# A convolution feeding a mixture of experts on one core: blocks of inner units taken in pairs over two PSUM banks for the tiles of chunks 6 to 21, and TensorE's subtraction kept to chunks 0 to 4

## The chip, the cores and the metric

The kernel runs on one core of a Trainium2 chip. The metric is the device time of one execution in microseconds (us). Engines are called as the profile calls them: PE is TensorE, DVE is VectorE, ACT is ScalarE, POOL is GpSimd, SP is SyncE.

## The reference

There are 8 x 3584 = 28672 tokens of width D = 192. First each token becomes a weighted sum over itself and the six tokens ahead of it (a convolution with its own seven weights for each token and head). Then the token is sent to one of eight experts, and the expert's output is scaled by the gate:

```
w = exp(w - max(w)); w /= sum(w)                      # 7 taps per token and head
x[s, h] = sum over k of w[s, h, k] * x_in[s - 6 + k, h]
logits = x @ w_gate                                    # 8 experts
e = argmax(logits);  p = softmax(logits)[e]
y = p * (relu(x @ w1[e]) @ w2[e])                      # 192 -> 1024 -> 192
```

## The kernel before

**Two halves that run side by side.** The tokens are cut into 28 chunks (numbers 0 to 27) of 1024 tokens. For each chunk the *convolution half* multiplies and adds the taps (`tap_ops`: rows named tv and acc at L386 and L410, nearly all of it on DVE from chunk 5 on), splits the sums into two float16 parts (`split`: pl at L498 and L500 on DVE, transposes L506 on PE, copies xg L508 on ACT), computes logits (L518 on PE), routes (`finish`: about twenty small DVE instructions, rank matmuls L545 and L547 on PE) and scatters each token's row into its expert's queue in DRAM (L589 on POOL). Each chunk then fixes which rows the next *tiles* take (`choose`, `rows` L615). A tile is up to 384 tokens of one expert. From chunk 5 on a chunk sets free two or three tiles.

**The expert half** (`experts`) takes one tile at a time. SP reads the tile's row number and fetches its tokens (xt), the expert's weights (wt) and the gate values (meta). The 1024 inner units are 8 blocks (NF) of 128. For each block of a tile of 384, PE runs five matmuls into a PSUM bank (ph, L890), ACT takes the relu as float16 (hh, L910), and the rest of the float32 value, relu(ph) - hh, is stored as a second float16 (hl). There are two ways to get hl. In the *DVE way* (`lo`) DVE computes it from ph and hh (L913). In the *PE way* (`rest`) PE subtracts hh in the bank with one more matmul per block (negi, L903), and ACT takes the relu of what is left (L905; hh is then at L899). The second layer (`l2`) is 24 matmuls for each 128 tokens (L787, 72 for a tile of 384); they belong to the tile before the current one and are issued between the current tile's blocks. ACT scales the result (o, L791) and POOL scatters it to the output.

**PSUM.** Of eight banks, four hold `ps_h`: the blocks ph, and also the transposes of `split`, take turns in them. One bank holds the weights wp of the taps, one (`ps_m`, pm) the logits and ranks, two (`ps_o`) the second layer's sums.

**Order.** DVE's instructions stand in the order in which the program writes them. A planner in the launch code keeps two clocks, `clock[0]` for DVE and `clock[1]` for PE; DVE steps of the convolution half are issued while DVE's clock is behind, and an hl is issued once its planned time is due, or at the latest when more than three wait (`pend`). A tile's start is not planned before the time at which its rows were chosen plus 16 us (FETCH). `finish` of a chunk is planned to begin REST1 = 6 us after its transposes. PE's and ACT's orders are those that the scheduler chose when the program was built. All five orders are fixed in the built program.

In the kernel before, the PE way is used for the tiles of chunks 0 to 5, and for every eighth tile of chunks 18 to 24.

Of the kernel before, what the change touches and what calls it, by code (L numbers as in the profile page):

```python
# [10 lines left out]
F32 = mybir.dt.float32  # L11
F16 = mybir.dt.float16
# [7 lines left out]
P = 128  # L20
# [3 lines left out]
NF = F // P  # L24
# [95 lines left out]
def conv_moe_kernel(ctx: ExitStack, tc: tile.TileContext, x, wgen, w_gate, w1, w2, out):  # L120
# [17 lines left out]
    pay = conv_pools.enter_context(tc.tile_pool(name="pay", bufs=1, side="right"))  # L138
    ps_h = ctx.enter_context(tc.tile_pool(name="ps_h", bufs=4, space=bass.MemoryType.PSUM))
    ps_w = ctx.enter_context(tc.tile_pool(name="ps_w", bufs=1, space=bass.MemoryType.PSUM))  # L140
    ps_m = ctx.enter_context(tc.tile_pool(name="ps_m", bufs=1, space=bass.MemoryType.PSUM))
    start_pools = ExitStack()
    ps_y = start_pools.enter_context(tc.tile_pool(name="ps_y", bufs=2, space=bass.MemoryType.PSUM))

# [348 lines left out]
    def low(c):  # L493
# [341 lines left out]

    pend = []
    lates = []

    def experts():
# [4 lines left out]
        left = 0  # L844
        subs = []
        loaded = {}
# [18 lines left out]
        while True:  # L865
# [10 lines left out]
            hl = ffh.tile([P, NF, T], F16, name="hl", padded_shape=[P, NF, T_MAIN])  # L876
            fg = max(g for g in (1, 2, 4, 8) if g * T <= 512 or g == 1)
            groups = NF // fg
            for t in range(groups):
# [3 lines left out]
                flush()  # L883
                while len(pend) > 3:
                    low_part()
                ph = ps_h.tile([P, fg, T], F32, name="ph")
                for g in range(fg):
                    f = f0 + g
                    for k, (wc, xc) in enumerate(((0, 0), (0, 2), (O_L0, 0), (O_H1, 1), (O_L1, 1))):
                        nc.tensor.matmul(ph[:, g], wt[:, wc + f * P:wc + (f + 1) * P], xt[:, xc, 0:T],  # L890
                                         start=(k == 0 and g == 0), stop=(k == 4),
                                         skip_group_check=g > 0)
                hv, lv = hh[:, f0:f0 + fg], hl[:, f0:f0 + fg]
                while subs:
                    subs.pop(0)()
                if ((n % 8 == 1 and todo[n][3] >= LATE_SUBS) or todo[n][3] < SUBS) and todo[n][3] < NCH - 3:


                    nc.scalar.activation(hv, ph, AF.Relu, scale=SHRINK)  # L899

                    def rest(ph=ph, hv=hv, lv=lv, fg=fg):
                        for g in range(fg):
                            nc.tensor.matmul(ph[:, g], negi, hv[:, g], start=False, stop=True,  # L903
                                             skip_group_check=True)
                        nc.scalar.activation(lv, ph, AF.Relu)  # L905
# [3 lines left out]
                else:  # L909
                    nc.scalar.activation(hv, ph, AF.Relu)  # L910

                    def lo(ph=ph, hv=hv, lv=lv):
                        nc.vector.scalar_tensor_tensor(lv, ph, 0.0, hv, op0=ALU.max, op1=ALU.subtract)  # L913
                        return (T * fg + 60) / 960.0

                    cost = T * fg * (5 + 4.5) / 2400.0 + 14 * fg * MM
                    clock[1] += cost
                    pend.append((clock[1] + LATE, n, lo))
# [6 lines left out]
                if t == groups - 1:  # L925
                    p = min(P, T)
# [7 lines left out]
            while subs:  # L934
                subs.pop(0)()
            second(10 ** 6)
# [9 lines left out]
    def last_tiles():  # L946

        loads = [fetch(len(todo) + i) for i in range(2)]
        for i in range(len(rest)):
# [9 lines left out]
            for f0 in range(0, NF, fg):  # L959
                ph = ps_h.tile([P, fg, T], F32, name="ph")  # L960
                for g in range(fg):
# [15 lines left out]
    def low_part():  # L977
        at, _, lo = pend.pop(0)
        clock[0] = max(clock[0], at) + lo()
# [101 lines left out]
    start_pools.close()  # L1081
    ps_o = ctx.enter_context(tc.tile_pool(name="ps_o", bufs=1, space=bass.MemoryType.PSUM))
    for i in range(2):
# [49 lines left out]
```

## Time and profile before

| | us |
|---|---|
| median of 3 runs | 1186.59 (1183.4 to 1188.95) |
| the profiled execution | 1185.47 |
| its span, first to last instruction | 1183.8 |
| PE busy | 1123.8 (95%) |
| DVE busy | 1034.9 (87%) |
| POOL busy | 696.3 (59%) |
| ACT busy | 647.1 (55%) |

Busy time is the sum of an engine's recorded instructions without overlap. Matmuls are pipelined: one is recorded longer than the distance to the start of the next, so a PE that shows no idle time may still be read only by counting its matmuls.

### The profile page before, as it was taken

What the parts mean: (1) busy time and instruction counts of PE and PEld (TensorE: products, weight loads), DVE (VectorE), ACT (ScalarE), POOL (GpSimd) and SP (SyncE); (2) the same over time, 40 slices, a digit from 0 to 9 for tenths busy, and PEclk for the clock granted to TensorE, in tenths of its full rate; (3) what the DMA queues carried; (4) which work ended last, traced back from release to release, by engine and by line L of the source; (5) the groups of instructions that cost most, each with busy time, mean ns of one, the idle gap of its engine ahead of it and who ended that gap; (6) DMA issues with size and microseconds to landing.
All of it is one profiled execution on the core that took longest, in us unless ns stands there. A gap on an engine that the chain in (4) does not pass through costs nothing. (4 is left out here: it accounts for less than half of the span.)

```text
span 1183.8 us, 29289 instructions
## 1 busy us (share of the span) xinstructions
PE 1123.8 (95%) x11327; PEld 913.1 (77%) x11327; DVE 1034.9 (87%) x1771; ACT 647.1 (55%) x1348; POOL 696.3 (59%) x633
## 2 busy tenths in 40 slices
PE   5689799999999999999999999999999999999996
PEld 3455489998778878787788888787777777778996
DVE  7999999999999999999999999999999997833231
ACT  3555477777556555545554555656465556443342
POOL 7998647766654654664566566447555675721222
PEclk9999899999999999999999999999999999999999
DMA  9989899999889787888898788777687666799993
GB/s 280 378 299 335 248 335 308 307 307 307 254 219 279 239 257 229 258 240 232 221 290 237 209 276 260 234 209 236 235 242 245 196 151 223 235 330 353 351 344 136
DMA packets 182847, 311.44 MB, mean 263 GB/s; under 512 B 131243, under 2 KB 154785, under 8 KB 167470
## 3 DMA queue, kind: packets, MB, share of 16 engines
q1 hardware_dynamic: 160702, 264.17, 73.3%
q0 software_dynamic: 22000, 45.33, 12.0%
q8 instruction: 91, 1.49, 0.5%
q14 instruction: 54, 0.44, 0.1%
HBM read 226.97 MB, written 60.45 MB: 243 GB/s over the span
## 5 line engine op out<-in xcount | busy, mean ns | idle before, releaser
L890 PE MATMUL ph<-xt,wt 128*128 128x384 f16 (+6 forms) x3680 | 571.2, 296 | 9.5 <-DVE hl L913 5.5
L787 PE MATMUL yo<-wt,hh 128*128 128x192 f16 (+1 forms) x3648 | 489.8, 246 | 2.9 <-ACT o L791 2.9
L589 POOL DMA_INDIRECT out_dram<-o,meta x228 | 281.1, 1233 | 323.5 <-ACT o L791 254.5
L787 PE MATMUL yo<-wt,hl 128*128 128x192 f16 (+1 forms) x1824 | 438.3, 246 | 0.0
L890 PEld LDWEIGHTS <-wt 128*128 128x128 f16 x3680 | 317.7, 98 | 124.3 <-issue 6.4
L910 ACT ACTIVATE hh<-ph 128x384 f16<-128x384 f32 (+2 forms) x485 | 238.5, 495 | 292.9 <-PE ph L890 272.1
L913 DVE SCALAR_TENSOR_TENSOR hl<-ph,hh 128x384 f16<-128x384 f32 (+2 forms) x485 | 260.4, 552 | 110.7 <-ACT hh L910 110.2
L787 PEld LDWEIGHTS <-hh 128*128 128x128 f16 (+1 forms) x3648 | 330.2, 98 | 32.9 <-issue 3.7
L589 POOL DMA_INDIRECT queue<-pl,pos x224 | 289.7, 1293 | 98.6 <-issue 72.9
L386 DVE TENSOR_TENSOR tv<-x_sb,wp 128x1536 f32<-128x1536 f32 (+1 forms) x173 | 286.2, 1656 | 1.7 <-PE ph L395 1.4
L410 DVE TENSOR_TENSOR acc<-acc,tv 128x1536 f32<-128x1536 f32 x138 | 239.6, 1736 | 0.0
L787 PEld LDWEIGHTS <-hl 128*128 128x128 f16 (+1 forms) x1824 | 178.7, 98 | 18.5 <-ACT hl L905 0.2
L791 ACT ACTIVATE o<-yo,fac 128x192 f32<-128x192 f32 (+1 forms) x228 | 90.5, 418 | 89.5 <-PE yo L787 85.1
L508 ACT ACTIVATE xg<-ph 128x1024 f16<-128x1024 f16 x84 | 81.6, 1022 | 38.2 <-PE ph L506 38.0
L395 PE MATMUL ph<-tv,identf 128*128 128x384 f32 x210 | 82.6, 539 | 17.8 <-DVE tv L386 17.1
L395 PEld LDWEIGHTS ph<-tv,identf 128*128 128x128 f32 x210 | 41.4, 209 | 45.2 <-DVE tv L386 19.0
L899 ACT ACTIVATE hh<-ph 128x512 f16<-128x512 f32 (+1 forms) x88 | 48.9, 562 | 22.1 <-PE ph L890 16.0
L447 ACT ACTIVATE junk<-x_sb 128x768 bf16<-128x768 f32 (+2 forms) x56 | 48.0, 857 | 16.1 <-DVE ssq L456 6.0
L905 ACT ACTIVATE hl<-ph 128x512 f16<-128x512 f32 (+1 forms) x88 | 47.7, 559 | 10.6 <-PE ph L903 10.2
L506 PE MATMUL ph<-idh,pl 128*128 128x128 f16 x672 | 52.3, 219 | 0.4 <-DVE pl L500 0.3
L486 ACT ACTIVATE pl<-acc 128x768 f16<-128x768 f32 (+1 forms) x51 | 39.0, 805 | 15.3 <-DVE acc L410 9.2
L506 PEld LDWEIGHTS <-pl 128*128 128x128 f16 x672 | 42.7, 98 | 5.9 <-ACT pl L491 2.6
(133 smaller groups left out, 768.9 us busy)
## 6 DMA issues: line engine op xcount, KB each, us to landing
wt<-wq SPq DMA_DIRECT2D x92, 1796.0 KB
x_sb<-in_x_dram SPq DMA_DIRECT2D x27, 1344.0 KB
w_sb<-in_weight_gen_dram SPq DMA_DIRECT2D x28, 224.0 KB
wq<-ws SPq DMA_DIRECT2D x8, 772.0 KB
f<-in_moe_w_dram SPq DMA_DIRECT2D x8, 768.0 KB
f<-in_moe_w_dram SPq DMA_DIRECT2D x8, 512.0 KB
wq<-ws SPq DMA_DIRECT2D x8, 512.0 KB
wq<-ws SPq DMA_DIRECT2D x32, 128.0 KB
```

The source lines that it names most:

```text
L386: eng.tensor_tensor(out, xs, ws, op=ALU.mult)
L395: nc.tensor.matmul(ap[:, 0:m], identf, tf[:, 2 * i * D:2 * i * D + m], start=(n == 0), stop=(n == KW - 1))
L410: eng.tensor_tensor(ac, ac, t, op=ALU.add)
L506: nc.tensor.transpose(pt[:, m, :], p16[:, j, n * P:(n + 1) * P], idh)
L508: nc.scalar.activation(k.xg[:, i:i + 8, :], pt, AF.Copy)
L589: st = nc.gpsimd.indirect_dma_start(out=dst, out_offset=bass.IndirectOffsetOnAxis(ap=idx, axis=0), in_=src, in_offset=None, **kw)
L787: nc.tensor.matmul(y, hx[:, f, sl], w2v[:, f, t, :], start=(f == 0 and k == 0), stop=(f == NF - 1 and k == 2))
L791: nc.scalar.activation(o[0:m, :], y, AF.Copy, scale=fac[0:m, s:s + 1])
L890: nc.tensor.matmul(ph[:, g], wt[:, wc + f * P:wc + (f + 1) * P], xt[:, xc, 0:T], start=(k == 0 and g == 0), stop=(k == 4), skip_group_chec ...
L899: nc.scalar.activation(hv, ph, AF.Relu, scale=SHRINK)
L910: nc.scalar.activation(hv, ph, AF.Relu)
L913: nc.vector.scalar_tensor_tensor(lv, ph, 0.0, hv, op0=ALU.max, op1=ALU.subtract)
```

## The change

Tiles of chunks 6 to 21 take two blocks at a time. A buffer is then a pair of banks (two pairs instead of four single banks), PE fills it with ten matmuls, ACT takes one relu over 768 columns and DVE one hl over 768 columns. Tiles of other chunks keep one bank at a time. The pools change over at the first tile of chunk 6 and at the first tile of chunk 22. While pairs are in use, the transposes go through the single bank of pm, and `finish` is planned 13 us (REST2) after the transposes instead of 6. The PE way is kept for chunks 0 to 4 alone. Rules for the order of l2's matmuls and of waiting hl's are adapted. Line numbers rise: L910 becomes L936, L913 becomes L939, L386 and L410 become L390 and L414, L508 becomes L513.

```diff
-SUBS = 6
-LATE_SUBS = 18
+SUBS = 5
+PAIRS_FROM = 6
+PAIRS_TO = 22
+REST2 = 13.0
...
         for i in range(0, len(blocks), 8):
-            pt = ps_h.tile([P, 8, P], F16, name="ph")
+            pt = (ps_m.tile([P, 8, P], F16, name="pm") if len(pairs) == 1 else
+                  (pairs[-1] if pairs else ps_h).tile([P, 8, P], F16, name="ph"))
...
-        yield max(0.0, ch[c].sent + REST1 - clock[0])
+        yield max(0.0, ch[c].sent + (REST2 if len(pairs) == 1 else REST1) - clock[0])
...
-            fg = max(g for g in (1, 2, 4, 8) if g * T <= 512 or g == 1)
+            sub_all = todo[n][3] < SUBS
+            stage_ = (todo[n][3] >= PAIRS_FROM) + (todo[n][3] >= PAIRS_TO)
+            if stage_ > len(pairs):
+                while pend:
+                    low_part()
+                flush_subs()
+                h_pools.close()
+                pairs.append((h_pools if stage_ == 1 else ctx).enter_context(tc.tile_pool(name=f"ps_d{stage_}", bufs=2 * stage_,
+                                                                space=bass.MemoryType.PSUM)))
+            nb = 2 if len(pairs) == 1 else 1
+            per = max(g for g in (1, 2, 4) if g * T <= 512 or g == 1)
+            fg = min(NF, per * nb)
...
-                while len(pend) > 3:
+                while len(pend) > 4 // nb - 1:
                     low_part()
...
-                if ((n % 8 == 1 and todo[n][3] >= LATE_SUBS) or todo[n][3] < SUBS) and todo[n][3] < NCH - 3:
+                if sub_all:
...
-                if t > 0 or groups == 1:
-                    while pend and pend[0][1] < n:
+                if t > 0 or groups == 1 or nb == 2:
+                    m = -(-left // (groups - t))
+                    if t == 0 and groups > 1:
+                        m = min(m, 3 * ready)
+                    while pend and pend[0][1] < n and (3 * ready < m or t > 0 or pend[0][3]):
                         low_part()
-                    m = -(-left // (groups - t))
```

In the stretch with pairs, ACT's order shows what became of the relu's and of the transposes. Here are ACT's rows late in that stretch in the changed program (hh and its bank ph, o with the second layer's bank yo, xg copied out of pm):

```order
L936 ACTIVATE hh_12377<-ph_12440 128x768
L796 ACTIVATE o_12458<-yo1_1337,fac_12183 128x192
L513 ACTIVATE xg_12474<-pm_12475 128x1024
L936 ACTIVATE hh_12377<-ph_12515 128x768
L513 ACTIVATE xg_12474<-pm_12485 128x1024
L796 ACTIVATE o_12539<-yo1_1337,fac_12183 128x192
L936 ACTIVATE hh_12377<-ph_12555 128x768
```

Before, each of these relu's was two rows of 128x384, and the three copies xg of a chunk read ph and stood next to each other; now they read pm, one after another in the same bank, with other work between them.

The second place is the third tile after the change back to single banks, which is also the first tile of the next chunk's rows. These are DVE's rows around the first hl of that tile (hl_14473) in the program before; acc and tv are the convolution of 1536 columns:

```order
L913 SCALAR_TENSOR_TENSOR hl_14201<-ph_14435,hh_14200 128x384
L534 SCALAR_TENSOR_TENSOR pri_14466<-lg_14409,revE_101 128x64
L459 TENSOR_SCALAR ssi_14468<-ssq_14461 128x1
L410 TENSOR_TENSOR acc_14146<-acc_14146,tv_14411 128x1536
L537 TENSOR_REDUCE pmx_14484<-pri_14466 128x8
L463 TENSOR_SCALAR rsx_14486<-ssi_14468 128x1
L386 TENSOR_TENSOR tv_14488<-x_sb_12894,wp_14147 128x1536
L540 TENSOR_TENSOR oh0_108<-pri_14466,pmx_14484 128x64
L554 TENSOR_REDUCE se_14551<-eg0_112 128x8
L466 TENSOR_SCALAR lsc_14553<-ssi_14468,gofs_172 128x1
L410 TENSOR_TENSOR acc_14146<-acc_14146,tv_14463 128x1536
L913 SCALAR_TENSOR_TENSOR hl_14473<-ph_14477,hh_14472 128x384
```

And these are DVE's rows at the same tile (its hl is hl_13967) in the changed program, with the middle of the stretch left out:

```order
L939 SCALAR_TENSOR_TENSOR hl_13638<-ph_13822,hh_13637 128x384
L414 TENSOR_TENSOR acc_13707<-acc_13707,tv_13817 128x1536
L939 SCALAR_TENSOR_TENSOR hl_13638<-ph_13840,hh_13637 128x384
L530 TENSOR_REDUCE lg_13891<-pm_13866 128x64
L390 TENSOR_TENSOR tv_13893<-x_sb_12418,wp_13708 128x1536
L533 TENSOR_REDUCE lm_13895<-lg_13891 128x8
L414 TENSOR_TENSOR acc_13707<-acc_13707,tv_13860 128x1536
...
L390 TENSOR_TENSOR tv_13984<-x_sb_12418,wp_13708 128x1536
L575 TENSOR_TENSOR rk_13980<-rk_13980,oh0_108 128x64
L370 RECIPROCAL sm_13978<-sm_13978 128x64
L414 TENSOR_TENSOR acc_13707<-acc_13707,tv_13913 128x1536
L939 SCALAR_TENSOR_TENSOR hl_13967<-ph_13971,hh_13966 128x384
```

Before, ten rows, three of them tv or acc, stand between the last hl of one tile and the first of the next. Now 27 rows stand there, from lg to acc: eight of them are tv or acc, and nineteen are small instructions of a chunk's routing and weights.

## Rows read from the trace of the kernel before

**Rows 1.** Busy time by stretch: the stretch, its length, then for PE, PEld (weight loads), DVE, ACT and POOL the busy us and in brackets the number of instructions, then the granted TensorE clock, the DMA share and GB/s.

```profile
core 0: us, PE busy (x) PEld busy (x) DVE busy (x) ACT busy (x) POOL busy (x), PEclk, DMA share, GB/s
0.00:150.00 150.00, 111.10 (x725) 71.24 (x726) 133.81 (x237) 74.55 (x125) 125.96 (x161) 0.94 0.93 309
...
240.00:400.00 160.00, 160.00 (x1652) 134.18 (x1650) 159.29 (x266) 100.77 (x216) 98.79 (x81) 1.00 0.92 268
400.00:600.00 200.00, 199.72 (x1982) 159.97 (x1980) 196.06 (x332) 109.17 (x237) 112.92 (x96) 1.00 0.83 241
600.00:810.00 210.00, 209.93 (x2076) 168.27 (x2075) 205.60 (x340) 117.51 (x254) 126.66 (x99) 1.00 0.83 249
810.00:970.00 160.00, 153.78 (x1536) 122.25 (x1534) 156.97 (x260) 88.42 (x187) 98.10 (x78) 1.00 0.70 211
970.00:1184.00 214.00, 200.90 (x2350) 174.66 (x2348) 96.26 (x210) 90.09 (x204) 76.77 (x77) 0.99 0.87 279
```

**Rows 2.** What PE waited for between 810 and 970 us: the waiting line, what it waited for, us in total, times, the longest us.

```profile
PE ph L890 <- DVE hl L913: 3.1, 7, 0.9
PE yo L787 <- ACT o L791: 1.7, 4, 0.7
PE ph L890 <- DMA xt<-queue: 1.4, 1, 1.4
```

**Rows 3.** Groups of instructions by line and shape over the whole span: count, busy us and mean ns of one, idle us just before them and what ended it.

```profile
L890 PE MATMUL ph<-xt,wt 128*128 128x384 f16 x2400 | 455.4, 326 | 6.0 <-DVE hl L913 4.4 <-DMA xt<-queue 1.4
L903 PE MATMUL ph<-hh,negi 128*128 128x384 f16 x32 | 9.6, 325 | 0.0
L913 DVE SCALAR_TENSOR_TENSOR hl<-ph,hh 128x384 f16<-128x384 f32 x451 | 237.9, 543 | 54.9 <-ACT hh L910 54.7
L913 DVE SCALAR_TENSOR_TENSOR hl<-ph,hh 128x512 f16<-128x512 f32 x29 | 19.9, 691 | 46.7 <-ACT hh L910 46.5
L910 ACT ACTIVATE hh<-ph 128x384 f16<-128x384 f32 x451 | 219.1, 489 | 270.2 <-PE ph L890 259.3 <-PE yo L787 5.6 <-issue 1.1
L910 ACT ACTIVATE hh<-ph 128x512 f16<-128x512 f32 x29 | 17.1, 598 | 21.6 <-PE ph L890 11.7 <-PE yo L787 10.0
L508 ACT ACTIVATE xg<-ph 128x1024 f16<-128x1024 f16 x84 | 81.6, 1022 | 38.2 <-PE ph L506 38.0
L350 DVE TENSOR_REDUCE mx<-w_sb 128x64 f32<-128x448 f32 x27 | 16.2, 602 | 0.0
L364 DVE TENSOR_REDUCE sm<-ew 128x64 f32<-128x512 f32 x28 | 18.7, 669 | 4.0 <-ACT ew L356 4.0
L366 DVE RECIPROCAL sm<-sm 128x64 f32<-128x64 f32 x28 | 15.1, 538 | 0.1
```

**Rows 4.** Pieces of the chain that ended last: start us, us, what (x and the number of instructions that follow each other). They give the distance from one instruction's start to the next.

```profile
722.25 0.93 DVE hl L913 x2
735.48 1.66 DVE tv L386
741.67 1.24 PE yo L787 x15
757.95 1.62 PE ph L890 x10
817.26 1.67 DVE acc L410
994.86 0.84 PE ph L506 x15
...
998.44 0.39 PE pm L518 x16
```

**Rows 5.** In order of time, ACT's relu of a block and DVE's hl of the same block, at a place where DVE waited for it: start us, us, engine, line, what, and in brackets the idle time before and what ended it.

```profile
408.48 0.49 ACT L910 ACTIVATE hh<-ph 128x384 f16<-128x384 f32 x1 [1.12 <-PE ph L890]
409.01 0.56 DVE L913 SCALAR_TENSOR_TENSOR hl<-ph,hh 128x384 f16<-128x384 f32 x1 [1.76 <-ACT hh L910]
```

**Rows 6.** DVE in order of time: small instructions of routing and the next large one's start.

```profile
883.86 0.15 DVE L615 TENSOR_SCALAR rows<-top 1x8 int32<-1x8 f32 x1
883.92 0.28 DVE L616 SCALAR_TENSOR_TENSOR key<-key,top,free 1x72 f32<-1x72 f32 x1
884.13 0.54 DVE L913 SCALAR_TENSOR_TENSOR hl<-ph,hh 128x384 f16<-128x384 f32 x1
...
884.73 1.20 DVE L498 TENSOR_TENSOR pl<-acc,pl 128x1024 f16<-128x1024 f32 x1
885.87 0.54 DVE L913 SCALAR_TENSOR_TENSOR hl<-ph,hh 128x384 f16<-128x384 f32 x1
886.33 0.67 DVE L500 TENSOR_TENSOR pl<-acc,pl 128x512 f16<-128x512 f32 x1
886.93 1.74 DVE L386 TENSOR_TENSOR tv<-x_sb,wp 128x1536 f32<-128x1536 f32 x1
...
899.85 0.22 DVE L530 TENSOR_TENSOR lg<-lg,lm 128x64 f32<-128x64 f32 x1
899.98 0.15 DVE L456 TENSOR_REDUCE ssq<-ssqs 128x1 f32<-128x8 f32 x1
900.05 1.74 DVE L386 TENSOR_TENSOR tv<-x_sb,wp 128x1536 f32<-128x1536 f32 x1
```

**Rows 7.** PE in order of time: the first matmuls of the tile whose rows were chosen at 883.86 us (first row of rows 6).

```profile
898.69 0.25 PE L787 MATMUL yo<-wt,hl 128*128 128x192 f16 x1
900.35 0.97 PE L890 MATMUL ph<-xt,wt 128*128 128x384 f16 x5 [1.42 <-DMA xt<-queue]
```

More of the change, by code (lines that the diff above doesn't have):

```diff
@@ L138, in conv_moe_kernel @@
     pay = conv_pools.enter_context(tc.tile_pool(name="pay", bufs=1, side="right"))
-    ps_h = ctx.enter_context(tc.tile_pool(name="ps_h", bufs=4, space=bass.MemoryType.PSUM))
     ps_w = ctx.enter_context(tc.tile_pool(name="ps_w", bufs=1, space=bass.MemoryType.PSUM))
     ps_m = ctx.enter_context(tc.tile_pool(name="ps_m", bufs=1, space=bass.MemoryType.PSUM))
+    h_pools = ExitStack()
+    ps_h = h_pools.enter_context(tc.tile_pool(name="ps_h", bufs=4, space=bass.MemoryType.PSUM))
+    pairs = []
     start_pools = ExitStack()
-    ps_y = start_pools.enter_context(tc.tile_pool(name="ps_y", bufs=2, space=bass.MemoryType.PSUM))
+    ps_y = start_pools.enter_context(tc.tile_pool(name="ps_y", bufs=2, space=bass.MemoryType.PSUM, side="right"))
     queue = dram.tile([E * NCAP, ROW // 2], I32, name="queue")
@@ L836, in conv_moe_kernel, with flush_subs @@
     pend = []
+    subs = []
     lates = []
+    def flush_subs():
+        while subs:
+            subs.pop(0)()
     def experts():
@@ L844, in experts @@
         left = 0
-        subs = []
+        ready = 0
         loaded = {}
@@ L883, in experts @@
                 flush()
-                while len(pend) > 3:
+                while len(pend) > 4 // nb - 1:
                     low_part()
-                ph = ps_h.tile([P, fg, T], F32, name="ph")
+                if nb == 2:
+                    while subs and len(subs) + len(pend) > 1:
+                        subs.pop(0)()
+                pb = (pairs[-1] if pairs else ps_h).tile([P, nb, 512], F32, name="ph")
+                ph = pb[:, :, 0:per * T].rearrange("p b (q t) -> p b q t", q=per)
+                phs = [ph[:, g // per, g % per] for g in range(fg)]
                 for g in range(fg):
@@ L889, in experts, with rest @@
                     for k, (wc, xc) in enumerate(((0, 0), (0, 2), (O_L0, 0), (O_H1, 1), (O_L1, 1))):
[L890 to L895, printed above, removed]
-                if ((n % 8 == 1 and todo[n][3] >= LATE_SUBS) or todo[n][3] < SUBS) and todo[n][3] < NCH - 3:
+                        nc.tensor.matmul(phs[g], wt[:, wc + f * P:wc + (f + 1) * P], xt[:, xc, 0:T],
+                                         start=(k == 0 and g % per == 0), stop=(k == 4),
+                                         skip_group_check=g % per > 0)
+                hv, lv = (a[:, f0:f0 + fg].rearrange("p (b q) t -> p b q t", b=nb) for a in (hh, hl))
+                flush_subs()
+                if sub_all:
                     nc.scalar.activation(hv, ph, AF.Relu, scale=SHRINK)
-                    def rest(ph=ph, hv=hv, lv=lv, fg=fg):
+                    def rest(ph=ph, phs=phs, lv=lv, f0=f0, fg=fg, hh=hh):
                         for g in range(fg):
-                            nc.tensor.matmul(ph[:, g], negi, hv[:, g], start=False, stop=True,
+                            nc.tensor.matmul(phs[g], negi, hh[:, f0 + g], start=False, stop=True,
                                              skip_group_check=True)
@@ L910, in experts, with lo @@
                     nc.scalar.activation(hv, ph, AF.Relu)
-                    def lo(ph=ph, hv=hv, lv=lv):
+                    def lo(ph=ph, hv=hv, lv=lv, size=T * fg):
                         nc.vector.scalar_tensor_tensor(lv, ph, 0.0, hv, op0=ALU.max, op1=ALU.subtract)
-                        return (T * fg + 60) / 960.0
+                        return (size + 60) / 960.0
                     cost = T * fg * (5 + 4.5) / 2400.0 + 14 * fg * MM
                     clock[1] += cost
-                    pend.append((clock[1] + LATE, n, lo))
-                if t > 0 or groups == 1:
-                    while pend and pend[0][1] < n:
+                    pend.append((clock[1] + LATE, n, lo, f0 + fg < NF))
+                if t > 0 or groups == 1 or nb == 2:
[3 more added lines that the diff above has]
+                    while pend and pend[0][1] < n and (3 * ready < m or t > 0 or pend[0][3]):
                         low_part()
-                    m = -(-left // (groups - t))
                     second(m)
@@ L925, in experts @@
                 if t == groups - 1:
+                    ready = f0
                     p = min(P, T)
@@ L933, in experts @@
                         done_.append(m)
-            while subs:
-                subs.pop(0)()
+            flush_subs()
             second(10 ** 6)
@@ L959, in last_tiles @@
             for f0 in range(0, NF, fg):
-                ph = ps_h.tile([P, fg, T], F32, name="ph")
+                pb = pairs[1].tile([P, 1, 512], F32, name="ph")
+                ph = pb[:, 0, 0:fg * T].rearrange("p (g t) -> p g t", t=T)
                 for g in range(fg):
@@ L977, in low_part @@
     def low_part():
-        at, _, lo = pend.pop(0)
+        at, _, lo, _ = pend.pop(0)
         clock[0] = max(clock[0], at) + lo()
@@ L1081, in conv_moe_kernel @@
     start_pools.close()
-    ps_o = ctx.enter_context(tc.tile_pool(name="ps_o", bufs=1, space=bass.MemoryType.PSUM))
+    ps_o = ctx.enter_context(tc.tile_pool(name="ps_o", bufs=1, space=bass.MemoryType.PSUM, side="right"))
     for i in range(2):
```

1 line of the change is left out of this document (added).

## The prediction

> **What bounds the kernel now.** I read the busy time by stretch first, because the averages of the whole span hide where PE waits. From 240 to 810 us PE is busy 569.65 of 570 us, while DVE is idle 0.7, 3.9 and 4.4 us in the three rows, 9 us in all: PE sets the pace [rows 1]. That PE is really at its limit there is read from the chain: five times two matmuls of 384 columns follow each other in 1.62 us (162 ns each), fifteen of 192 columns in 1.24 us (82.5 ns) [rows 4]. From 810 to 970 us the roles change: DVE is idle 3.0 of 160 us, PE 6.2 us [rows 1], and the largest of PE's waits are for hl from DVE [rows 2]. The granted clock is 1.00, that is 2.4 GHz, in both stretches [rows 1], so nothing is to be had there. Before 150 us PE works 111 of 150 us on the start, and after 970 us DVE has only 96 us of work in 214 and PE runs the last tiles [rows 1]; the change's tables do not touch the start (its orders are the same up to the tiles of chunk 5) and hardly the end.
>
> So the kernel's time is PE's work plus PE's waits, and a microsecond of DVE work counts only where PE waits for DVE.
>
> **The PE way goes.** 32 matmuls of 384 columns, four tiles of eight blocks, leave PE [rows 3]. At 162 ns each (rows 4, as their form is that of L890) that is **-5.2 us**, on the path, since PE has no other idle time to fill. DVE gets 32 hl's in exchange, at 0.465 us from start to start (0.93 for two) [rows 4]: +14.9 us.
>
> **Pairs.** 344 hl's of 384 columns become 172 of 768. No row shows 768. From 384 to 512 columns an hl grows from 543 to 691 ns, 1.16 ns for each column [rows 3]; the convolution's 1536 columns in 1.66 us [rows 4] give 1.0 ns as the lower slope, with some 80 ns fixed. So an hl over 768 is spaced 0.86 to 0.91 us, against 0.93 for two, and the pairs save 20 to 70 ns each, 3.5 to 12 us in all. DVE's sum is thus +3 to +11 us. That DVE work lies in the stretch where DVE was idle 9 us anyway, and PE's waits there are nearly nothing, so I take 0 for what the pairs give back, with the gain of a rival below as the other bound. The Trainium skill's page "Perfetto Trace Analysis" (section Optimizing Scalar/DVE Operations) says that a DVE instruction on PSUM carries some 125 ns of its own, and that grouping pays if the engine is saturated. By that figure the pairs would save an estimated 21 us of DVE and DVE's sum would be -7 us; the rows above give at most 70 ns for it, and DVE is not the limit where the pairs are.
>
> ACT's relu goes from 489 ns for 384 columns to 598 for 512 [rows 3], 0.85 ns for each column, so about 0.82 us for 768; two rows cost 0.98. ACT is 55% busy in this stretch [rows 1], so 0.
>
> **What could hold PE in the pairs.** Between the last matmul into a pair and the first that needs its banks again PE's order has a median of 4.9 us of matmuls; seventeen of the 172 have less than 3.7, the least 1.8. What must happen in that time: about 0.16 us until the last sums are there (a matmul is recorded 326 ns and spaced 162 [rows 3, 4]), the relu 0.82, the hl 0.86 to 0.91, and one convolution instruction of 1.67 that may stand ahead of it: 3.5 to 3.6 us. So nearly all fit. The transposes are similar: pm comes back after its copy of 1.02 us [rows 3] and perhaps a relu of 0.82 ahead of it, 2.0 us with the 0.16, and the order has at least 1.9 us of PE work between, and over 2.2 in all but two cases. I take **+0.5 us** for all of this; the bounds are 0 and 8.5 us (half a microsecond at each of the seventeen). A pair's extra logic for l2's order and the two or three smaller groups in the last short tiles I take at 0; they lie under PE's matmuls, and uncovered the latter would cost three relu's, 1.5 us.
>
> **The waits of 810 to 970 us.** What the windows show as idle, 6.2 us, misses the part of a wait that lies under the record of the matmul ahead, about 0.16 us for each of the 12 waits [rows 2, 3]. So PE loses 8.1 us there now: **-8.1 us** if they all go, and then the new waits are added.
>
> **The hand-over back to single banks.** Here the order of DVE decides. In the changed program, at the third tile of single banks, 27 rows stand between the last hl of one tile and the first of the next. Eight are tv or acc at 1.66 to 1.67 us [rows 4], 13.3 us. Of the nineteen small ones three (mx, sm and its reciprocal) are 602, 669 and 538 ns long, which is 0.53, 0.59 and 0.46 from start to start if each overlaps the next by 75 ns as an hl does (543 against 465); the other sixteen are spaced like L615, L616, L530 and L456, 0.06 to 0.21, some 1.9 together [rows 3, 4, 6]. That is 16.8 us without an hl.
>
> I count from the last hand-over at which DVE must wait for PE, the fill of ph_13822 (seven microseconds of PE work without a fill stand ahead of it). DVE: 0.16 for the sums, 0.49 for the relu and 0.04 to the start of hl [rows 3 to 5], then hl 0.465, acc 1.67, hl 0.465, the 16.8, and the first hl of the next tile 0.465: 20.6 us. PE from the same point: 8 logit matmuls (24 ns each) and 5 of L1, 1.0 us; then 20 of L1 (3.2), 46 of l2 (3.8) and 17 small ones (0.4), after which it needs that hl's bank [rows 4]: 8.5 us. PE waits **12.1 us**. Until the last of the next eight hl's DVE does another 12.0 us (eight hl's 3.7, three convolution instructions 5.0, pl 1.14 and 0.60, eight small ones 1.6), and PE has 9.0 us (25 of L1, 44 of l2, 24 transposes at 56 ns) [rows 4, 6]: **3.0 us** more. Together **+15.1 us**, and DVE is behind PE by so much that no later place in the order makes PE wait again. In the program before, the same place has ten rows and three convolution instructions, 5.8 us by the same rows, and its waits are among the 8.1 that I took off.
>
> A second path ends at the same place. The rows of that tile are chosen about 7 us of PE work ahead of its first matmul. Before, at the same tile, 16.5 us passed from L615 at 883.86 to the first matmul at 900.35, which had to wait 1.4 us for xt [rows 6, 7]. So the fetch alone would hold PE for 9 to 10 us; it runs at the same time as DVE's 16.8 us, and adds nothing up to 15 us.
>
> **Sum.** -5.2 - 8.1 + 15.1 + 0.5 = +2.3 us, on the profiled execution's 1185.5 (its span 1183.8 and 1.7 around it) 1187.8. That execution lies 1.1 us under the median of the runs, so 1188.9: **1189 us**. I call a change of under 0.5% (5.9 us) no change: the runs shown differ by that much.
>
> **Rivals.**
> - *PE waits inside the pairs* (slower). Two banks come back together, later than one did. For it: the margin of 3.6 against 3.7 us at seventeen places, DVE 98% busy there [rows 1]. Against it: the median margin of 4.9, and each wait lets DVE catch up. With half a microsecond at each of the seventeen, +8.5 instead of +0.5: 1197 us. It decides from 3.6 us of such waits. The same page of the Trainium skill, in the same section, says that where ScalarE or VectorE is not saturated but causes bubbles elsewhere, breaking instructions up may let work finish sooner; that is this rival.
> - *DVE gets ahead* (faster). The pairs and the longer pause before routing leave DVE early at the change back, so that PE waits there no more than before: -5.2 alone is 1181.9; with no late waits at all 1173.6. For it: DVE's idle 9 us show that it has room. Against it: an idle DVE in a fixed order waits at an hl; it cannot begin the convolution that stands behind. It decides where the new wait is under 7 us.
> - *The fetch takes longer than before*, over 22 us from choosing to the first matmul, or the last chunk's 16 scatters start late, so that the first of the last tiles waits: +3 to +5 us more, 1192 to 1194.
> - That the change doesn't do what it says is out: the 172 wide rows and the missing 32 matmuls stand in the orders.
>
> **How the numbers follow.** The forecast has 0.60, the waits inside the pairs 0.18, the gain of DVE 0.12, the late fetch or tail 0.10. The forecast's own range is 1184 to 1194: the first wait alone (12.1) to both and 3 us of waits in the pairs. The range of 8 in 10 reaches from 1181.5, near the first of the faster cases, to 1197.5, the pairs' case. Over 0.5% faster is under 1180.7: half of the 0.12 and a little of the rest, 0.09. Over 0.5% slower is above 1192.5: nearly all of the 0.18, half of the 0.10 and a few hundredths of the forecast, 0.27. The rest is 0.64.
>
> **What would show it.** PE's records of L903 only for 256 columns, and hl of 768 columns at about 0.95 us; no PE wait over 0.3 us from 240 us up to the third single-bank tile (near 885 us); then, in about 25 us, PE idle of 12 to 15 us, on xt first, then on DVE's rank input and hl; after that DVE-made waits below 2 us until 970. The forecast is wrong if PE's idle time is spread over the pairs' stretch, or if the idle near 885 us is under 7 or over 20 us.

## The result, and the profile after

The changed kernel takes **1192.25 us** (median of 6 runs, 1188.92 to 1197.32), the kernel before 1185.11 (6 runs); the ratio is **1.0062**, 95% interval 1.0034 to 1.009. (The ratios here and below leave out executions in a slower state, so they can differ by up to some 0.5% from the quotient of the two medians.) That is 7.1 us more, 3 us above the 1189 that I had said. The ratio lies on the slower side of my bound of 0.5%, to which I had given 0.27, and its interval on both sides of it. The profiled execution is the slowest of the six: 1197.32 us, span 1195.5.

The busy time by stretch of the changed kernel, in the columns of [rows 1]:

```profile
core 0: us, PE busy (x) PEld busy (x) DVE busy (x) ACT busy (x) POOL busy (x), PEclk, DMA share, GB/s
240.00:400.00 160.00, 158.76 (x1641) 133.07 (x1639) 158.02 (x235) 91.76 (x173) 99.02 (x79) 1.00 0.95 269
400.00:600.00 200.00, 199.95 (x1981) 160.01 (x1979) 199.01 (x278) 102.95 (x177) 118.48 (x95) 1.00 0.79 245
600.00:810.00 210.00, 209.69 (x2085) 168.49 (x2084) 206.37 (x294) 108.44 (x186) 131.11 (x104) 1.00 0.79 245
810.00:970.00 160.00, 145.89 (x1441) 115.37 (x1440) 149.75 (x237) 77.03 (x152) 86.18 (x72) 0.97 0.67 207
970.00:1196.00 226.00, 210.24 (x2407) 182.45 (x2404) 104.54 (x227) 90.27 (x206) 81.06 (x79) 0.96 0.83 265
```

Through the stretch of pairs PE is idle 1.6 of 570 us; from 810 to 970 it is idle 14.1 us, where it was 6.2 [rows 1], and its clock is no longer 1.00. What it waited for there, as in [rows 2]:

```profile
PE ph L917 <- DMA wt<-wq: 6.4, 1, 6.4
PE ph L917 <- DVE hl L939: 6.2, 2, 4.9
PE yo L792 <- ACT o L796: 1.5, 3, 0.7
```

The groups by shape that answer to [rows 3]: hl and relu over 768 columns, and the PE way, of which only 256 columns are left.

```profile
L939 DVE SCALAR_TENSOR_TENSOR hl<-ph,hh 128x768 f16<-128x768 f32 x172 | 162.1, 942 | 4.6 <-ACT hh L936 4.5
L936 ACT ACTIVATE hh<-ph 128x768 f16<-128x768 f32 x172 | 138.9, 808 | 203.2 <-PE ph L917 199.3 <-DVE hl L939 2.9 <-issue 0.3
L929 PE MATMUL ph<-hh,negi 128*128 128x256 f16 x112 | 21.5, 272 | 0.0
```

Two of DVE's rows in order of time, of which the first is an hl over 768 columns. From its start to the next start it is 0.87 us, which is also the median of all that are followed without a wait:

```profile
561.87 0.94 DVE L939 SCALAR_TENSOR_TENSOR hl<-ph,hh 128x768 f16<-128x768 f32 x1
562.74 0.20 DVE L579 TENSOR_REDUCE pos<-rk 128x8 int32<-128x64 f32 x1
```

And the hand-over, the third tile of single banks, in order of time (start us, us, engine, line, what, and in brackets the idle time before and what ended it). PE:

```profile
895.04 0.49 PE L792 MATMUL yo<-wt,hh 128*128 128x192 f16 x4
901.93 5.53 PE L917 MATMUL ph<-xt,wt 128*128 128x384 f16 x20 [6.39 <-DMA wt<-wq]
908.35 0.64 PE L792 MATMUL yo<-wt,hh 128*128 128x192 f16 x4 [0.72 <-ACT o L796]
...
916.75 1.78 PE L917 MATMUL ph<-xt,wt 128*128 128x384 f16 x5 [4.90 <-DVE hl L939]
```

ACT and DVE at the same place:

```profile
907.49 0.49 ACT L936 ACTIVATE hh<-ph 128x384 f16<-128x384 f32 x1 [0.32 <-PE ph L917]
...
908.49 0.36 ACT L536 ACTIVATE eg<-lg,lsc 128x64 f32<-128x64 f32 x1
```

```profile
895.70 0.55 DVE L939 SCALAR_TENSOR_TENSOR hl<-ph,hh 128x384 f16<-128x384 f32 x1
...
905.40 0.21 DVE L545 TENSOR_TENSOR oh<-pri,pmx 128x64 f16<-128x64 f32 x1
908.87 0.23 DVE L559 TENSOR_REDUCE se<-eg 128x8 f32<-128x72 f32 x1 [3.25 <-ACT eg L536]
...
916.14 0.55 DVE L939 SCALAR_TENSOR_TENSOR hl<-ph,hh 128x384 f16<-128x384 f32 x1
```

Windows of one us there, in the columns of [rows 1]; the last column but two is the granted clock (0.50 is 1.2 GHz):

```profile
900.00:901.00 1.00, 0.00 (x0) 0.00 (x0) 1.00 (x3) 0.00 (x0) 0.00 (x0) 0.50 1.34 216
907.00:908.00 1.00, 0.62 (x5) 0.35 (x4) 0.00 (x0) 0.68 (x3) 0.00 (x0) 1.00 1.27 240
917.00:918.00 1.00, 1.00 (x4) 0.45 (x3) 1.00 (x1) 0.00 (x0) 0.39 (x1) 0.50 0.87 292
```

The reader is to see one chain. PE has nothing of this tile until its weights are there, at 901.93. Its 20 matmuls then take 5.53 us, where 20 times 162 ns and the rest of the last record are 3.4: the clock fell to its lower level while PE stood, and most of the 20 run at it. ACT works in order: eg, the exponential of another chunk's logits, stands behind the relu's of this tile and starts only at 908.49. DVE also works in order: the sum of eg stands ahead of two acc's, a tv and the first hl, so that DVE stands still for 3.25 us, and PE waits for that hl until 916.75. Without that wait the 27 rows take DVE 16.7 us, from 896.17 (0.47 after the start of the hl ahead of them) to the hl at 916.14.

**Where the time went.** By PE's loss I mean a stretch's length less what its matmuls need at the distances of [rows 4]: the idle time of the windows, 0.16 us under the record ahead of each wait, and what the lower clock adds. The last row runs to PE's last matmul.

| part | before | changed | difference |
|---|---|---|---|
| PE way gone: 32 matmuls of 162 ns | | | -5.2 |
| PE's loss up to 810 us | 94.6 | 95.2 | +0.6 |
| PE's loss 810 to 970 us | 8.5 | 19.2 | +10.7 |
| PE's loss after 970 us | 5.4 | 11.3 | +5.9 |
| sum | | | +12.0 |

Of the loss from 810 to 970 us, 18.5 us lie between 880 and 970 in the changed kernel, where the kernel before has 5.6. The spans differ by 11.7 us; what follows the last matmul is 0.2 us shorter than before. The medians differ by 7.1, so some 5 us belong to this one execution; which of the lines they are in, the trace of one execution can't say.

The last line of the table is in the last tiles. SyncE's last issue of weights comes 9.5 us later than before, and the last tile's first matmul stands the same 17.2 to 17.3 us behind it in both. The changed kernel's rows, then those of the kernel before:

```profile
1159.53 0.34 SPq L832 DMA_DIRECT2D wt<-wq  x1
...
1172.15 1.60 PE L917 MATMUL ph<-xt,wt 128*128 128x48 f16 x40 [2.02 <-SPq L1137]
1176.87 0.29 PE L917 MATMUL ph<-xt,wt 128*128 128x32 f16 x4 [3.10 <-SPq L1137]
```

```profile
1149.99 0.34 SPq L827 DMA_DIRECT2D wt<-wq  x1
...
1167.18 0.27 PE L890 MATMUL ph<-xt,wt 128*128 128x32 f16 x4 [1.46 <-SPq L1108]
```

PE, 5.4 us later than before at 1160 (its work and losses up to there), so runs into two waits of 5.1 us together where there was one of 1.5, and its granted clock is lower at the end (0.62):

```profile
1170.00:1180.00 10.00, 4.87 (x65) 4.58 (x64) 0.71 (x2) 1.37 (x4) 0.91 (x1) 0.62 0.47 195
```

### The profile page after: what moved, and what is told of

Read it like the earlier page. It is cut to its first block, busy times and chain, and to the rows that moved or that the text cites. A ratio compares the mean times of both kernels' runs of the same rounds, so it can differ in the third digit from the quotient of the medians.

```text
span 1195.5 us, 28894 instructions
## 1 busy us (share of the span) xinstructions
PE 1124.7 (94%) x11295; PEld 913.8 (76%) x11295; DVE 1038.8 (87%) x1634; ACT 612.4 (51%) x1147; POOL 699.3 (58%) x633
## 3 DMA queue, kind: packets, MB, share of 16 engines
q0 software_dynamic: 22000, 45.33, 11.7%
## 4 chain that ended last, share of the span: by engine, by line
PE 70%; DVE 11%; DMA 10%; issue 4%; POOL 2%; ACT 1%; SPq 1%; POOLq 0%; DVEq 0%; ACTq 0%
PE ph L917 33%; PE yo L792 30%; DMA wt<-wq 5%; DVE tv L390 3%; DVE hl L939 2%; DMA f<-in_moe_w_dram 2%; DVE acc L414 2%; PE ph L399 2%; PE pm L511 1%; PE pm L523 1%; PE ph L511 1%; DMA x_sb<-in_x_dram 1%; PE ph L929 1%; POOL out_dram L594 1%; DMA w_sb<-in_weight_gen_dram 1%
## 5 line engine op out<-in xcount | busy, mean ns | idle before, releaser
L917 PE MATMUL ph<-xt,wt 128*128 128x384 f16 (+6 forms) x3680 | 558.8, 298 | 20.5 <-DVE hl L939 7.6
L594 POOL DMA_INDIRECT out_dram<-o,meta x228 | 293.4, 1287 | 326.0 <-ACT o L796 260.4
L917 PEld LDWEIGHTS <-wt 128*128 128x128 f16 x3680 | 322.0, 98 | 148.4 <-DMA wt<-wq 8.8
L936 ACT ACTIVATE hh<-ph 128x768 f16<-128x768 f32 (+4 forms) x348 | 226.8, 653 | 336.3 <-PE ph L917 314.3
L939 DVE SCALAR_TENSOR_TENSOR hl<-ph,hh 128x768 f16<-128x768 f32 (+4 forms) x348 | 259.7, 751 | 114.5 <-ACT hh L936 112.9
L594 POOL DMA_INDIRECT queue<-pl,pos x224 | 280.8, 1254 | 109.9 <-issue 77.6
L390 DVE TENSOR_TENSOR tv<-x_sb,wp 128x1536 f32<-128x1536 f32 (+1 forms) x173 | 285.9, 1655 | 2.3 <-PE ph L399 1.9
L414 DVE TENSOR_TENSOR acc<-acc,tv 128x1536 f32<-128x1536 f32 x138 | 239.3, 1734 | 0.0
L399 PE MATMUL ph<-tv,identf 128*128 128x384 f32 x210 | 82.4, 538 | 17.2 <-DVE tv L390 16.5
L513 ACT ACTIVATE xg<-ph 128x1024 f16<-128x1024 f16 x42 | 41.1, 1022 | 26.5 <-PE ph L511 26.4
L513 ACT ACTIVATE xg<-pm 128x1024 f16<-128x1024 f16 x42 | 42.9, 1023 | 17.3 <-PE pm L511 17.1
L925 ACT ACTIVATE hh<-ph 128x512 f16<-128x512 f32 x56 | 33.2, 601 | 14.1 <-PE ph L917 8.5
L390 DVE TENSOR_TENSOR acc<-x_sb,wp 128x1536 f32<-128x1536 f32 x23 | 39.9, 1735 | 0.0
```

The source lines that it names most:

```text
L390: eng.tensor_tensor(out, xs, ws, op=ALU.mult)
L399: nc.tensor.matmul(ap[:, 0:m], identf, tf[:, 2 * i * D:2 * i * D + m], start=(n == 0), stop=(n == KW - 1))
L414: eng.tensor_tensor(ac, ac, t, op=ALU.add)
L594: st = nc.gpsimd.indirect_dma_start(out=dst, out_offset=bass.IndirectOffsetOnAxis(ap=idx, axis=0), in_=src, in_offset=None, **kw)
L917: nc.tensor.matmul(phs[g], wt[:, wc + f * P:wc + (f + 1) * P], xt[:, xc, 0:T], start=(k == 0 and g % per == 0), stop=(k == 4), skip_group_ ...
```

## The experiments

My theory after this profile was that the loss lies in DVE's order at the hand-over, made longer by the fetch through ACT. Its parts and rivals: *fetch holds DVE* (the weights come late, and eg with them), *REST2 makes the gap* (the later start of routing puts 27 rows without an hl there), *the missing help* (the late tiles of the PE way spared DVE 24 hl's, 11.2 us at 0.465, and PE must now wait for that sum). Twelve runs of seven kernels followed. In the first nine, on three chips, the kernel before itself took 1283 to 1298 us; of these only the ratio to the kernel before, measured beside them, is used. The last three (their labels begin with h and i) met the kernel before at 1187 to 1189.

**The changed kernel itself, among the first nine.**

> The changed kernel itself once more, beside the kernel before: the measure for the experiments on this chip. On a chip where the kernel before takes about 1185 us I expect the ratio of the first comparison, 1.006 (1.003 to 1.009). On a chip that is slow for all kernels (before about 1283 us, idle time that waits for nothing the profile shows), the same kernel with only the fetch of one tile reordered took 0.993 twice; if that reordering is worth the 3.3 us of 'fetch holds DVE', the changed kernel itself is at 0.995 there; if it is worth nothing, at 0.993; if it is above 1.000, the reordering is worth more than 8 us there. In each of the cases below 1, the sign of the change hangs on the chip, and what the change wins there is not among the terms of my sum.

1292.75 us against 1298.09, ratio **0.996** (0.9925 to 0.9996): the sign is turned. The span of its profile is 95 us longer than that of the profile above. Of these, 43 us are idle time of PE that waited for nothing the profile shows ("issue"), in 61 waits, where the profiles of the two kernels by the result above have none; the rest I did not take apart:

```profile
PE yo L792 <- issue: 22.7, 33, 1.8
...
PE ph L917 <- issue: 11.8, 15, 2.5
...
PE pm L523 <- issue: 7.0, 10, 1.2
```

The instructions themselves are as long as ever (tv 1.74 us, hl over 768 columns 0.95). With such holes on PE, a place where it must wait for DVE's sum would be worth less; that is argued, not shown, since no profile of the kernel before was taken beside it. Why the holes come and go is open: one of these chips gave 1285 us for the kernel before in the first four runs and 1189 under three hours later.

**The fetch of the hand-over tile.** In fetch, for tile 60 alone, wt is issued ahead of xt; every other engine's rows stay where they were.

```diff
+        if n == 60:
+            wt = pw.tile([P, WROW], F16, name="wt")
+            nc.sync.dma_start(wt, wq[ds(e * P, P), :])
         xt = px.tile([P, 3, T_MAIN], F16, name="xt", bufs=AHEAD if ring else 3)
         rows_of(nc.sync.dma_start_transpose(xt[:, :, 0:T], q16[ds(r, T), 0:2 * D]))
-        wt = pw.tile([P, WROW], F16, name="wt")
-        nc.sync.dma_start(wt, wq[ds(e * P, P), :])
+        if n != 60:
+            wt = pw.tile([P, WROW], F16, name="wt")
+            nc.sync.dma_start(wt, wq[ds(e * P, P), :])
```

> The changed kernel with one edit: for the tile that waits at the hand-over (the third of single banks) the fetch of the weights wt is put ahead of the gather xt in SP's queue, as it already stands in the program before; every row of PE, ACT, DVE and GpSimd stays where it was. Theory 'fetch holds DVE': in the changed kernel wt was issued at 893.53, behind an xt that waited until 891.89 for the scatters, PE started at 901.93, and ACT's eg stood behind the relu of that tile, so that DVE sat idle 3.25 us. With wt issued near 887, PE starts that tile 3 to 6 us earlier (before, 3.9 us passed from the issue of xt to the first matmul: 891.89 + 3.9 = 895.8), DVE's wait for eg is gone, and PE's loss at the hand-over falls from 18.5 us to about 15: 3.3 us less than the changed kernel, 1188 to 1189.5. Rival 'the rows decide' (DVE's 27 rows alone, the fetch in parallel, as I had predicted): the first wait moves from wt to hl, nothing is won, 1192. Rival 'the fetch decides': the whole 6 us are won, 1186.

1274.62 against 1285.44: 0.993 (0.9885 to 0.9967).

> The kernel of e1_wt60 once more (on the chip of the first four runs the kernel before itself took 1285 us, with idle time on all engines that waited for nothing the profile shows, so that a difference of 3 us cannot be read there). Against a kernel before of about 1185 us: theory 'fetch holds DVE', PE starts the third tile of single banks 3 to 6 us earlier, DVE's 3.25 us wait for eg is gone, PE's loss at the hand-over falls from 18.5 to about 15 us, time 1188 to 1189.5 (ratio 1.003); rival 'the rows decide', nothing is won, 1192 (1.006); rival 'the fetch decides', 1186 (1.001).

1274.86 against 1282.84: 0.993 (0.9897 to 0.9954). Against 0.996 of the changed kernel (another chip) this is nothing that can be told apart.

> The kernel of e1 and f1 (wt ahead of xt in SP's queue for the tile of the hand-over, nothing else) beside the kernel before at about 1185 to 1189 us. Theory 'fetch holds DVE': PE starts the third tile of single banks 3 to 6 us earlier, DVE's 3.25 us wait for eg is gone or under 1 us, PE's loss at the hand-over 15 us in place of 18.5; ratio 1.003 in place of 1.006. Rival 'the rows decide': 18 us stay, ratio 1.006. Rival 'the fetch decides': the whole 6 us are won, ratio 1.001.

1196.03 against 1186.91: **1.0082** (1.0062 to 1.0102). Nothing is won, but not for the reason that any of the three gives. SyncE, GpSimd, PE and DVE of this kernel at the hand-over (L917 is L921 here):

```profile
888.04 0.33 SPq L831 DMA_DIRECT2D wt<-wq  x1
897.53 1.33 SPq L833 DMA_TRANSPOSE xt<-queue  x1
```

```profile
888.82 0.96 POOL L594 DMA_INDIRECT queue<-pl,pos  x1 [0.31 <-DMA queue<-pl,pos]
...
897.47 0.14 POOL L476 IOTA pl<- 128x8 int32 x1 [5.11 <-DMA queue<-pl,pos]
```

```profile
901.05 5.69 PE L921 MATMUL ph<-xt,wt 128*128 128x384 f16 x20 [5.41 <-DMA xt<-queue]
```

```profile
908.16 0.23 DVE L559 TENSOR_REDUCE se<-eg 128x8 f32<-128x72 f32 x1 [2.43 <-ACT eg L536]
```

The weights left at 888.04 instead of 893.53, as wanted. But xt may go only when the chunk's scatters have landed. The last of these was issued at 888.82 here and 888.71 in the changed kernel; there xt went at 891.89, here at 897.53. With 1.8 MB of weights sent ahead of it the scatter landed over 5 us later. So PE started 0.88 us earlier and not 3 to 6. What the run does show is the coupling: PE 0.88 earlier, DVE's wait for eg 0.82 shorter (2.43 for 3.25), PE's loss from 880 to 970 us 17.6 for 18.5.

**The later start of routing.** REST2 = 6.0 in place of 13.0, one line.

> The changed kernel with REST2 = 6.0, as REST1: the later start of routing while pairs are in use is undone, pairs and the shorter PE way stay. At the third tile of single banks 15 rows of DVE with 7 of tv or acc now stand without an hl, where there were 27 with 8: about 13 us where there were 16.8. wt also stands ahead of xt there. Theory 'REST2 makes the gap': about 4 us less by the rows and 3.3 less by the fetch, 1184 to 1186, PE's loss between 880 and 970 about 11 us. Rival 'the missing help' (DVE has 24 hl's, 11.2 us, more to do there since the late tiles lost their PE way, and PE waits for that sum wherever the gap is): the waits are only spread over 880 to 970, and the time stays within 2 us of the changed kernel's 1192.

1350.0 against 1285.44: 1.056 (1.0495 to 1.0615).

> The kernel of e2_rest6 once more (there it took 1.056 of the kernel before; its profile had waits of PE for hl of 51 us, the changed kernel's had 6.5 between 240 and 1000). Against a kernel before of about 1185 us: theory 'REST2 makes the gap', 1184 to 1186; rival 'the missing help', within 2 us of 1192. A third case, opened by that run: with routing started early, pairs and routing rows collide through the whole stretch of pairs, and PE waits for hl there too: 1200 or more. Then the later start of routing is what lets pairs run without waits.

1348.83 against 1282.84: 1.052 (1.0471 to 1.0567). The third case. What DVE waited for from 360 to 960 us, here and then in the changed kernel where it was at 0.996:

```profile
DVE lg L530 <- PE pm L523: 95.2, 13, 12.6
```

```profile
DVE lg L530 <- PE pm L523: 12.7, 8, 3.7
```

DVE stands 95 us for the logits, and PE then 43.5 us for hl. How that comes about is seen in the last experiment, one of the last three.

**The late tiles of the PE way given back.**

```diff
-            sub_all = todo[n][3] < SUBS
+            sub_all = todo[n][3] < SUBS or (n % 8 == 1 and 18 <= todo[n][3] < NCH - 3)
```

> The changed kernel with the late PE way given back: tiles 1 of 8 from chunk 18 on are subtracted by TensorE as before (three tiles, 24 matmuls of 384 columns, 3.9 us of PE); pairs and REST2 stay. Theory 'the missing help': DVE loses 24 hl's (11.2 us) before the hand-over and in it, so PE's loss at 880 to 970 falls from 18.5 us to 5 or less; net of 3.9 us that is 8 to 11 us less than the changed kernel: 1181 to 1184, faster than before. Rival 'REST2 makes the gap': gaps of 26 rows still stand in DVE's order, so the waits stay above 12 us, and with 3.9 us more of PE work the time is 1192 to 1196.

1267.97 against 1285.44: 0.987 (0.9811 to 0.9929).

> The kernel of e3_subs_back once more (there it took 0.987 of the kernel before, interval 0.981 to 0.993, on a chip on which all kernels were slow). Against a kernel before of about 1185 us: theory 'the missing help', PE's loss between 880 and 970 us falls from 18.5 us to 5 or less, net of 3.9 us of TensorE work 8 to 11 us less than the changed kernel, 1181 to 1184 (ratio 0.996 to 0.999); rival 'REST2 makes the gap', waits above 12 us stay, 1192 to 1196 (1.006 to 1.009).

1258.73 against 1282.84: 0.981 (0.9767 to 0.9846).

> The kernel of e3 and f2 (the late PE way given back, pairs and REST2 as in the change) once more, since h1_late_rest met a chip on which the kernel before takes 1188.8 us. In h1 PE lost 26 us from 700 to 880 us, with DVE standing 29.6 us in 8 waits for the logits, from the chunk on at which routing started early again; up to there PE lost 1.7 us. With REST2 kept, those waits should be gone (in the changed kernel they are 2.7 us in all from 240 to 890). Theory 'the missing help': PE's loss between 880 and 970 us is 5 us or less where the changed kernel's is 18.5; ratio 0.992 to 0.997. Rival 'REST2 makes the gap': gaps of 26 rows stand in DVE's order here too, waits above 12 us, ratio 1.006 to 1.009.

1182.26 against 1186.91: **0.9966** (0.9949 to 0.9984), faster than both kernels. Its window and PE's waits from 810 to 970 us:

```profile
810.00:970.00 160.00, 157.21 (x1568) 124.95 (x1566) 155.94 (x245) 84.75 (x165) 92.31 (x77) 1.00 0.72 219
```

```profile
PE yo L792 <- ACT o L796: 1.2, 2, 0.7
PE ph L917 <- DVE hl L939: 1.1, 1, 1.1
```

PE idles 2.8 us where the changed kernel idles 14.1, the clock stays at 1.00, and its loss from 880 to 970 us is 4.3 for 18.5; 3.9 us of matmuls buy this. REST2 is as in the change, so REST2 alone doesn't make the loss. Rows of DVE without an hl, 26 of them, stand in this order too; but those stand at tiles of the PE way, at which PE waits for no hl, and at the hand-over tile only 13 rows stand, three of them tv or acc. The kernel before is alike: its 27 rows from 859.8 to 876.4 us stand at a tile of the PE way. Whether the 11.2 us fewer or the place of the long pieces does it, the run doesn't separate: the planner makes both out of one edit.

**Only the PE way cut, in the kernel before** (SUBS = 5, no late tiles; single banks, REST1).

> The kernel before with only the PE way cut as in the change (up to chunk 4, no late tiles), single banks and REST1 throughout. PE loses 32 matmuls of 162 ns, 5.2 us; DVE gets 32 hl's of 0.465 us, 14.9 us, of which about 4.5 fit where DVE was idle. Theory 'the missing help': PE waits for DVE in the last third rise by 10 to 14 us over those of before, time 1190 to 1194: the cut of the PE way alone makes the kernel slower, and pairs and REST2 only give a little back or nothing. Rival 'REST2 and the hand-over make the loss': without them the cut is a gain or nothing, 1180 to 1186.

1282.25 against 1285.44: 1.000 (0.9962 to 1.0038). The loss of 5 to 9 us that *the missing help* expected is not there, as its rival had it. But it was run only among the first nine, where the change itself is at 0.996; what the cut alone does where the kernel before takes 1185 us stays open.

**Late PE way and earlier fetch together** (the two edits above, the fetch for tiles 60 to 73).

> Two edits of the earlier runs together: the late PE way is given back (tiles 1 of 8 from chunk 18) and the fetch of wt is put ahead of xt for the tiles 60 to 73, pairs and REST2 as in the changed kernel. By 'the missing help' and 'fetch holds DVE' together PE's loss between 880 and 970 us is below 5 us, with no wait for wt or for DVE of more than 2 us. Against a kernel before of about 1185: 1178 to 1182 (ratio 0.994 to 0.998). On a slow chip as that of the first runs: at or below the 0.981 and 0.987 of the late PE way given back alone. Rival (either edit's worth is used up by the other, or the last tiles' transfers set the end anyway): no better than the late PE way alone.

1281.04 against 1298.09: 0.986 (0.9811 to 0.9911), no better than the late PE way alone (0.987 and 0.981, on other chips): the rival is borne out.

**Late PE way, and routing early again from chunk 19 on.** This was to be the best. Both edits are in this kernel; the second is

```diff
-        yield max(0.0, ch[c].sent + (REST2 if len(pairs) == 1 else REST1) - clock[0])
+        yield max(0.0, ch[c].sent + (REST2 if len(pairs) == 1 and c < 19 else REST1) - clock[0])
```

> The changed kernel with the late PE way given back, and with routing started at REST1 again from chunk 19 on (REST2 for the pairs of chunks 6 to 18 only). Of the 26- and 27-row stretches of DVE without an hl only those at tiles of the PE way stay, at which PE waits for no hl. On a chip where the kernel before takes about 1185 us: PE's loss between 880 and 970 about 2 us, 3.9 us of TensorE work given back, 1176 to 1180 (ratio 0.993 to 0.996), the best of all. On a slow chip: if the early start of routing is what cost 1.052 in f3_rest6 in all chunks of pairs alike, three of sixteen chunks with it cost about 1% there, so 0.990 to 0.997 against the 0.981 to 0.987 of the late PE way given back alone; if the cost of the early start lies in the first chunks only, 0.980 to 0.987.

1205.32 against 1188.84: **1.0146** (1.0121 to 1.0172), some 22 to 26 us above the ratios expected. The windows before and from the place where routing starts early, and what DVE and PE waited for in the second:

```profile
240.00:680.00 440.00, 439.25 (x4439) 358.82 (x4437) 433.43 (x621) 235.87 (x422) 271.50 (x213) 1.00 0.85 254
680.00:880.00 200.00, 184.92 (x1766) 144.38 (x1764) 172.37 (x242) 94.36 (x161) 104.70 (x90) 0.96 0.73 224
```

```profile
DVE lg L530 <- PE pm L523: 25.6, 5, 6.1
```

```profile
PE ph L917 <- DVE hl L939: 13.8, 9, 2.9
```

A chunk on the way from its split to its logits: here DVE's last pl and first row of routing, then PE's transposes and logit matmuls, and last DVE's two rows for a chunk in the changed kernel:

```profile
730.74 0.66 DVE L504 TENSOR_TENSOR pl<-acc,pl 128x512 f16<-128x512 f32 x1
...
742.76 0.29 DVE L530 TENSOR_REDUCE lg<-pm 128x64 f32<-128x128 f32 x1 [4.22 <-PE pm L523]
```

```profile
733.14 0.55 PE L511 MATMUL pm<-idh,pl 128*128 128x128 f16 x7
...
736.48 0.61 PE L511 MATMUL pm<-idh,pl 128*128 128x128 f16 x8
...
739.21 0.61 PE L511 MATMUL pm<-idh,pl 128*128 128x128 f16 x8
741.97 0.75 PE L523 MATMUL pm<-gw,xg 128*128 128x16 f16 x24
```

```profile
565.15 0.67 DVE L504 TENSOR_TENSOR pl<-acc,pl 128x512 f16<-128x512 f32 x1
...
579.97 0.27 DVE L530 TENSOR_REDUCE lg<-pm 128x64 f32<-128x128 f32 x1
```

With pairs all transposes go through the one bank pm, in three trips with a copy by ACT between, 3 us apart; from the end of pl (731.4) to the end of the logits (742.7) 11.3 us pass. DVE asks after REST1, about 7 us, and stands 4.2 us, with the convolution and the next hl behind it. With REST2 it asks 14 us after pl and doesn't wait. So REST2 is not a cost of the change but the cover that pairs need; without it PE's loss between 680 and 890 us is 26.5 us, where the changed kernel has 1.5 and the kernel with the late PE way, which differs by REST2 alone, 0.7.

## Why the prediction was right, and where not

- *The PE way goes, -5.2*: the 32 matmuls are gone (L929 has 256 columns only). What I did not see is that most of the loss that I put down to the hand-over comes with them: given back, the late ones cost 3.9 us and return 14.2 us of loss between 880 and 970 us. The two ratios, 1.0062 and 0.9966, each to the kernel before beside it, put 0.96% on this one edit.
- *Pairs*: hl over 768 columns is 942 ns long and spaced 0.87 us (561.87 to 562.74), as worked out (0.86 to 0.91), against 0.93 for two; the relu 808 ns (0.82). The Trainium skill's page "Perfetto Trace Analysis" (section Optimizing Scalar/DVE Operations) gives some 125 ns of overhead for each DVE instruction on PSUM. The trace does not agree: one instruction fewer saves 60 ns here, and the measurement decides. Waits in the pairs: 0.36 us of idle from 400 to 810, and 1.24 from 240 to 400, where two waits (0.6 for wt, 0.4 for an o) are over the 0.3 that I had set as a sign. The rival of waits in the pairs is out, but only because REST2 came with them.
- *Waits of 810 to 970 go, -8.1; the hand-over, +15.1*: the place and the order (first a transfer, then hl) are as predicted; I had named xt, and it was wt. DVE's 27 rows took 16.7 us without their wait, where I had 16.8. The idle time seen is 14.1 us, with 0.16 for each of six waits 15.1, but that it equals my 15.1 is luck: the loss from 880 to 970 us is 18.5, because some 3.7 us of it came as matmuls at the lower clock and not as waits.
- *The second path "adds nothing up to 15 us"* is the step that failed. The bound was for the time that the fetch holds PE, 22 us from the choice of rows as the rival has it. The fetch stayed well within it: from the choice of rows (886.62) to the first matmul 15.3 us passed, and PE was held 6.4. It added all the same, since the two paths are not parallel: ACT's order ties DVE to the fetch. The 20 matmuls took 2.1 us longer than at 2.4 GHz, before ACT came to eg, and DVE lost 3.25 us. 15.1 + 3.25 is 18.4, the loss measured 18.5. The run with wt ahead agrees with the tie, 0.82 us of DVE for 0.88 of PE; it is one execution against one.
- *The clock* had no term. At 2.4 GHz throughout 810 to 970 us before [rows 1], it fell to 1.2 GHz twice, during the waits of 6.4 us and of 4.9 us, and cost PE 2.1 us in the 20 matmuls and 1.5 us in those from 916.75 to 920.4.
- *The last tiles* I took at nothing, and put "+3 to +5" into a rival of 0.10. They came to +5.9 in this execution, which is its slowest; that the last weights are issued 8 to 10 us later stands in both profiles with that hand-over (1159.53 and, with wt ahead, 1158.41, against 1149.99; with the late PE way back 1147.36).
- *DVE gets ahead* (faster): it would have needed a wait under 7 us; out. (Its 1173.6 should be 1173.8, which is 1181.9 less 8.1.)

The time thus lies inside my range, but in part by luck. The medians rose by 7.1 us where the sum had +2.3, and the profiled execution, at 1197.32, lies outside the range of 1184 to 1194. Against the sum the stretch from 810 to 970 us was short by 3.7 (10.7 for 15.1 - 8.1), the start and the pairs by 0.1, and the end by what part of 5.9 is in a median execution. That part stays open.

## What to carry to other kernels

Work that one engine does for another is worth what it saves at the place where the other is waited for: the same 24 matmuls that cost 3.9 us of the busiest engine saved 14. Two paths that meet are added as parallel only after one has looked whether an engine that works in order (here ACT, with eg behind the relu) carries both. And before a delay constant is called a loss, look what it covers: REST2 hid the longer way over one bank.

## What was not expected of the hardware

- In waits of 6.4 us and 4.9 us the granted clock of PE fell to 1.2 GHz, and the next matmuls ran at it for some us (20 in 5.53 us for 3.4; 5 in 1.78 for 0.97).
- 1.8 MB of weights sent 0.8 us ahead of a scatter's last instruction put off the gather that waits for that scatter from 3.2 to 8.7 us after it.
- The same kernel took 1285 us and, under three hours later, 1189 on the same chip. The four kernels profiled beside the first have 41 to 48 us of PE idle time that waits for nothing shown ("issue"), the one profiled beside the second has none. Among the runs with such idle time the sign of the change turned (0.996 for 1.0062).
